# An attention, Fourier and feed-forward kernel on one core: value rows copied by ScalarE or VectorE, with a new order of all steps

## The chip, the core and the metric

The kernel runs on one core of one Trainium2 chip. The metric is the device time of one execution in microseconds (us); the time before is the median of three runs. Each engine (TensorE, VectorE, ScalarE, GpSimd, and SyncE, which issues most transfers) has its own instruction stream, and the streams meet only where one waits for another's result.

## The reference, cut to what is computed

```python
def _attn_ref(q, k, v):                      # q, k, v: (8, 8, 576, 64) float32
    scores = scale * np.matmul(q, k.transpose(0, 1, 3, 2))
    mask = (rel >= 0) & (rel < 64)           # each row sees its last 64 positions
    ...                                      # softmax
    return np.matmul(attn, v).astype(np.float32)

def _moe_ref(x, w_ch1, w_ch2):               # x: (8, 576, 512), weights float64
    X = np.fft.fft(np.fft.fft(x, axis=1), axis=2)
    u = x + np.real(X).astype(np.float32)
    ...                                      # un: u, normalized over its last axis
    ch = np.maximum(un @ w_ch1, 0.0) @ w_ch2   # 512 to 2048 and back to 512
    return (u + ch).astype(np.float32)
```

## The kernel before

The 4608 rows are cut into 36 tiles of 128 rows (T = 0 to 35, nine to a pair of batches). Each tile goes through attention (`attn_tile`); when the four and a half tiles of a batch are done, `fft` transforms that batch, `norm_tile` gathers the transformed rows, adds and normalizes them, and `ffn` and `ffn7` run the two feed-forward products on chunks of two tiles (c = 0 to 17). Tiles 0 to 12 (`T < PRO`, in the code `whole`) do attention in float32; later tiles split each float32 into two float16 parts. The weights come as float64 and are loaded, converted and squared (`weight_piece`), then scaled and split.

In attention a row sees only 64 positions, so each tile needs its own value rows and those of the tile before. There are two buffers `va` (`vbuf[0:2]`) that hold a tile's 128 value rows as loaded, each with 65 columns a head (64 values and a one), and two buffers `ve` (`vbuf[2:4]`): `v_own` (L624) copies the first 64 partitions of `va` to the tile's `ve`, and `v_next` (L632) copies the last 64 partitions to the `ve` of the next tile. One such copy is 64 partitions by 520 float32. Both are issued by SP as transfers for all tiles; for tile 12, `v_next` is two VectorE operations (L629, L630) that also split into parts. The products with the values (L739, `pa`) read `va` and `ve`.

Every step is recorded with `op(engine, duration, due time, function, reads, writes, alt=...)`. Nothing is emitted then: `Plan.follow` walks the list `ORDER`, which names all 3,023 steps by number, and this order is the order of each engine's stream. Where a step has an alternative engine (`alt`), it takes the second one if its number is in the set `SECOND`. So the two tables are a schedule written out by hand, and an engine that meets a step whose data are late holds all steps behind it. Where the plan foresees that TensorE will stand for over 0.8 us before the feed-forward products, dummy matmuls are put in (`warm`, L1551).

Names that the prediction uses: L516 loads of query, key and value rows (`qn`, `kn` in a ring of two buffers, `va`); L553 their transposes on TensorE; L486, L490, L496 helpers that copy or add on ScalarE, VectorE or any engine; L685 the exponentials on ScalarE; L1078 the gather; L1093 the first step of the normalization (`stats`); L1290 and L1271 the first and second feed-forward product of the float16 chunks and the one float32 chunk; L1299 and L1302 the two halves of the evacuation between them (ScalarE, then VectorE).

Of the kernel before, what the change touches and what calls it, by code (L numbers as in the profile page):

```python
# [382 lines left out]
def attn_fft_ffn_kernel(ctx: ExitStack, tc: tile.TileContext, q, k, v, w1, w2, gidx, dft_d, dft_s, mask, out):  # L383
# [116 lines left out]
    def attn_tile(T, base):  # L500
# [125 lines left out]
        def v_next():  # L626
# [4 lines left out]
            else:  # L631
                nc.sync.dma_start(vbuf[3 - i][64:128], vbuf[i][64:128])  # L632

        op("DMA", 0.55, base - 4 if whole else base + 3.2, v_own, [Bva[i]], [Bve[i]], lat=2.8)
        if n + 1 < NT and T + 1 == PRO:
            op("DVE", 1.1, base + 6, v_next, [Bva[i]], [Bve[1 - i]])
        elif n + 1 < NT:
# [945 lines left out]
```

## Time and profile before

| | us |
|---|---|
| median of 3 runs (lowest to highest) | 983.53 (983.04 to 984.14) |
| profiled execution | 983.49 |
| its span, first to last instruction | 981.7 |
| TensorE busy | 950.0 |
| VectorE busy | 740.5 |
| ScalarE busy | 395.6 |
| GpSimd busy | 350.4 |

The profile is one execution. A busy share counts instructions that work; the granted clock is the TensorE clock that the chip allowed, as a share of 2.4 GHz (1.00 and 0.50 are its two levels). The chain of waits is followed back from the last instruction: at each step to what released it. A table of windows gives each engine's busy time in stretches of the span, counted from its start.

### The profile page before, as it was taken

The numbers are of one execution on the slowest core, as the hardware profiler recorded it, in microseconds if no ns is written. First come the engines' busy times: TensorE is split into PE (matmuls) and PEld (weight loads), VectorE is DVE, ScalarE is ACT, GpSimd is POOL, SyncE is SP. The second block draws the span as 40 slices with busy tenths as digits, with TensorE's granted clock in tenths as the row PEclk, the third lists the DMA queues.
The fourth block names the chain that finished last, engine by engine and source line by source line (L and its number), as shares of the span: only waits on it lengthen the run. The fifth ranks groups of instructions, "written<-read, shape, count | busy, mean of one in ns | idle before, by whom it ended". The sixth has DMA issues, their size and how long they took to land.

```text
span 981.7 us, 23698 instructions
## 1 busy us (share of the span) xinstructions
PE 950.0 (97%) x9259; PEld 707.4 (72%) x9259; DVE 740.5 (75%) x2036; ACT 395.6 (40%) x895; POOL 350.4 (36%) x684
## 2 busy tenths in 40 slices
PE   7789999999999999999999899999999999999997
PEld 6566768666776767666776567666776668888887
DVE  4789898989768677765765758777889999774645
ACT  4555566843452244333442224323442324232321
POOL 0254133344452552525542223334353323232221
PEclk9899999999999999999999899999999999999999
DMA  8978764625779848699668638567863500211100
GB/s 183 214 215 237 190 192 119 152 66 109 167 169 169 156 104 159 141 177 159 135 154 144 129 86 145 122 146 154 153 123 86 104 12 28 63 36 50 25 23 23
DMA packets 309073, 123.16 MB, mean 125 GB/s; under 512 B 291096, under 2 KB 291224, under 8 KB 308960
## 3 DMA queue, kind: packets, MB, share of 16 engines
q1 hardware_dynamic: 306240, 112.72, 54.0%
q0 software_dynamic: 2720, 8.92, 3.3%
q8 instruction: 73, 1.20, 0.5%
q14 instruction: 40, 0.33, 0.1%
HBM read 54.99 MB, written 14.17 MB: 70 GB/s over the span
## 4 chain that ended last, share of the span: by engine, by line
PE 74%; DVE 10%; DMA 8%; POOL 4%; issue 2%; ACT 1%; SPq 1%; DVEq 0%; POOLq 0%; ACTq 0%
PE ph L1290 24%; PE po L1271 24%; PE ph L1429 7%; PE po L1415 7%; PE pa L739 2%; PE pz L1004 2%; PE pg L970 2%; PE psc L660 2%; DMA kn<-in_k 2%; DMA qn<-in_q 2%; DMA uhl<-up 1%; DVE td L1364 1%; DMA py<-yp 1%; POOL fs L496 1%; PE pp L696 1%
## 5 line engine op out<-in xcount | busy, mean ns | idle before, releaser
L1290 PE MATMUL ph<-uhl,w0s 128*128 128x256 f16 (+1 forms) x2616 | 331.1, 278 | 5.7 <-DVE hh L1302 4.7
L1271 PE MATMUL po<-w1s,hh 128*128 128x512 f16 (+1 forms) x1312 | 334.1, 391 | 1.8 <-DVE hh L1302 0.9
L1290 PEld LDWEIGHTS <-w0s 128*128 128x128 f16 x2496 | 243.8, 98 | 66.8 <-issue 7.1
L1271 PEld LDWEIGHTS <-hh 128*128 128x128 f16 x1248 | 119.6, 98 | 108.6 <-issue 2.2
L1299 ACT ACTIVATE hh<-ph 128x512 f16<-128x512 f32 x104 | 61.7, 595 | 174.5 <-PE ph L1290 122.5
L1302 DVE SCALAR_TENSOR_TENSOR hh<-ph,hh 128x512 f16<-128x512 f32 x104 | 71.2, 685 | 43.0 <-ACT hh L1299 42.8
L685 ACT ACTIVATE pr<-pr,nm 128x128 f32<-128x128 f32 x288 | 90.9, 390 | 24.0 <-DVE nm L677 23.9
L1429 PE MATMUL ph<-uhl,w0s 128*128 128x256 f16 x768 | 90.4, 273 | 0.2 <-DVE hh L1302 0.2
L677 DVE CUSTOM_DVE_ANT_0 pr<-psc,mskb 128x128 f32<-128x128 f32 x288 | 65.5, 284 | 25.8 <-PE psc L660 14.3
L1429 PEld LDWEIGHTS <-w0s 128*128 128x128 f16 x768 | 75.1, 98 | 10.1 <-issue 0.6
L496 POOL TENSOR_TENSOR flex<-pr,flex 128x128 f16<-128x128 f32 x88 | 41.8, 503 | 72.2 <-ACT flex L486 36.4
L1102 POOL TENSOR_TENSOR rs<-mv,mhalf 128x1 f32<-128x1 f32 x36 | 24.6, 684 | 117.7 <-DVE mv L1098 112.9
L1078 POOL DMA_INDIRECT mt<-md,gix x34 | 35.7, 1050 | 81.9 <-DMA md<-mp 28.3
L496 POOL TENSOR_TENSOR flex<-qn,flex 128x128 f16<-128x128 f32 x96 | 43.5, 486 | 18.6 <-ACT flex L486 10.4
L1415 PEld LDWEIGHTS <-hh 128*128 128x128 f16 x448 | 43.8, 98 | 5.1
L496 POOL TENSOR_TENSOR up<-un,up 128x128 f16<-128x128 f32 x64 | 29.8, 492 | 43.7 <-ACT up L486 26.5
L1440 ACT ACTIVATE hx<-ph 128x512 f32<-128x512 f32 x32 | 19.0, 596 | 60.9 <-PE ph L1429 46.4
L739 PE MATMUL pa<-ve,pt 128*64 128x65 f16 (+1 forms) x760 | 41.4, 207 | 1.5 <-DMA ve<-va 1.0
L739 PE MATMUL pa<-va,pt 128*64 128x65 f16 (+1 forms) x760 | 41.5, 207 | 0.0
L1453 DVE TENSOR_TENSOR hl<-hx,hh 128x896 f16<-128x896 f32 x27 | 29.4, 1092 | 13.2 <-ACT hh L486 12.7
L1445 DVE TENSOR_TENSOR hx<-hx 128x128 f32<-128x128 f32 x96 | 25.0, 303 | 18.7 <-ACT hx L1440 17.8
L496 POOL TENSOR_TENSOR hs<-h,hs 128x97 f16<-128x97 f32 x48 | 21.7, 484 | 47.9 <-ACT hs L486 40.5
(207 smaller groups left out, 1608.5 us busy)
## 6 DMA issues: line engine op xcount, KB each, us to landing
wd<-in_moe_w_ch SPq DMA_DIRECT2D x20, 512.0 KB, 4.7
out<-xu SPq DMA_DIRECT2D x36, 256.0 KB, 2.4
ve<-va SPq DMA_DIRECT2D x67, 130.0 KB, 3.5
kn<-in_k SPq DMA_DIRECT2D x32, 256.0 KB, 3.6
qn<-in_q SPq DMA_DIRECT2D x32, 256.0 KB, 4.2
flex<-in_moe_w_ch SPq DMA_DIRECT2D x12, 512.0 KB, 7.6
flex<-in_v SPq DMA_DIRECT2D x20, 256.0 KB, 3.3
md<-mp SPq DMA_DIRECT2D x24, 192.0 KB, 2.2
```

The lines of the kernel that those rows point to most:

```text
L496: eng.tensor_tensor(out=out[:, k : k + w], in0=in0[:, k : k + w], in1=in1[:, k : k + w], op=al)
L677: nc.vector.tensor_tensor_reduce(out=t["pr", g][:, hp], in0=t["ps", g][:, hp], in1=mskb[:, m : m + P], scale=-0.125, scalar=3.0e38, op0=AL ...
L685: nc.scalar.activation(pr, pr, AF.Exp, bias=t["nm", g][:, hp : hp + 1], scale=-1.0)
L739: nc.tensor.matmul(pa[sl, hp], pt[:, sl], v_, start=(x == 0), stop=(x == len(mm) - 1))
L1078: nc.gpsimd.indirect_dma_start(out=mts[T], out_offset=None, in_=mds[pb][0 : HR if n < 4 else 2 * HR], in_offset=bass.IndirectOffsetOnAxis( ...
L1271: nc.tensor.matmul(t["po"][i], l_, r_, start=(f == 0 and x == 0), stop=(f == NKF - 1 and x == len(mm) - 1))
L1290: nc.tensor.matmul(ph, l_, r_, start=(x == 0), stop=(x == len(mm) - 1))
L1299: nc.scalar.activation(t["hh", j][:, 0], ph, AF.Relu)
L1302: nc.vector.scalar_tensor_tensor(out=hh[:, 1], in0=ph, scalar=0.0, in1=hh[:, 0], op0=ALU.max, op1=ALU.subtract)
L1415: nc.tensor.matmul(t["po", bk][:, x], t["h", j][a][:, slot], right(n, j, b_), start=(j == 0 and k == 0 and n in (1, 7, 2, 5)), stop=(j == ...
L1429: nc.tensor.matmul(ph, l_, r_, start=(x == 0), stop=(x == len(mm) - 1))
L1453: eng.tensor_tensor(out=lo[:, a:b_], in0=x[:, a + 1 : b_ + 1], in1=hi[:, a:b_], op=ALU.subtract)
```

## The change

The 13 own copies and the 11 next copies of the float32 tiles that were transfers become steps of ScalarE, with VectorE as the alternative engine. The copies of the float16 tiles (43) stay transfers, and so do the loads.

```diff
-        op("DMA", 0.55, base - 4 if whole else base + 3.2, v_own, [Bva[i]], [Bve[i]], lat=2.8)
+        if whole:
+            op("ACT", 0.62, base - 4, lambda e: copy(e, vbuf[2 + i][0:64], vbuf[i][0:64]), [Bva[i]], [Bve[i]],
+               alt=("DVE", 0.36))
+        else:
+            op("DMA", 0.55, base + 3.2, v_own, [Bva[i]], [Bve[i]], lat=2.8)
         if n + 1 < NT and T + 1 == PRO:
             op("DVE", 1.1, base + 6, v_next, [Bva[i]], [Bve[1 - i]])
+        elif n + 1 < NT and whole:
+            op("ACT", 0.62, base - 3.9, lambda e: copy(e, vbuf[3 - i][64:128], vbuf[i][64:128]), [Bva[i]], [Bve[1 - i]],
+               alt=("DVE", 0.36))
         elif n + 1 < NT:
-            op("DMA", 0.55, base - 3.9 if whole else base + 6, v_next, [Bva[i]], [Bve[1 - i]], lat=2.8)
+            op("DMA", 0.55, base + 6, v_next, [Bva[i]], [Bve[1 - i]], lat=2.8)
```

`ORDER` and `SECOND` are replaced as a whole by tables from another search, in which transfers come late twice as often and long. The number of steps and their numbering stay. Of the 24 copies two are in the new `SECOND` (179, the next copy of tile 0, and 228, the own copy of tile 2); 22 are on ScalarE. 188 other steps change their engine, among them two key copies (tiles 0 and 3) to VectorE and three copies of transposed probabilities (tiles 0 and 3) to ScalarE before the first feed-forward matmul. The gather of tile 20 that the prediction speaks of is step 1324.

In the new list the first copies stand on ScalarE so, with the steps right behind them: own copy of tile 0, exponentials of tile 0; own copy of tile 3, exponentials of tile 3; next copies of tiles 4 and 3, exponentials of tile 4; own copy of tile 5, key copy of tile 6. Ahead of the first feed-forward matmul (step 369) the two lists hold the same 71 steps of TensorE; SP has 66 steps there before and 51 after.

## Rows read from the trace of the kernel before

**Rows 1.** The page: span; busy time and share of each engine; TensorE in 40 slices.
```profile
span 981.7 us, 23698 instructions
PE 950.0 (97%) x9259; PEld 707.4 (72%) x9259; DVE 740.5 (75%) x2036; ACT 395.6 (40%) x895; POOL 350.4 (36%) x684
...
PEclk9899999999999999999999899999999999999999
```

**Rows 2.** Windows: length, busy us of each engine (x instructions), granted clock, DMA share, GB/s.
```profile
0.00:90.00 90.00, 71.37 (x845) 56.11 (x845) 66.18 (x251) 48.09 (x129) 28.69 (x65) 0.92 0.88 218
90.00:130.00 40.00, 39.74 (x279) 28.16 (x280) 35.79 (x107) 23.70 (x66) 13.87 (x23) 1.00 0.70 186
130.00:500.00 370.00, 368.46 (x3632) 262.69 (x3631) 289.00 (x814) 167.76 (x378) 157.84 (x328) 1.00 0.69 144
500.00:560.00 60.00, 54.81 (x516) 37.71 (x514) 36.38 (x92) 16.20 (x38) 18.47 (x32) 0.94 0.70 140
560.00:955.00 395.00, 393.82 (x3797) 303.45 (x3796) 300.19 (x745) 136.16 (x281) 127.12 (x231) 1.00 0.41 86
955.00:982.00 27.00, 21.80 (x200) 19.29 (x198) 12.98 (x29) 3.69 (x6) 4.45 (x7) 0.97 0.06 21
```

**Rows 3.** Groups of TensorE: busy us, mean ns | idle before them.
```profile
L1551 PE MATMUL warm<-ident 128*128 128x256 f16 x87 | 15.1, 310 | 2.2 <-POOL ident masks.py:199 2.2
```

**Rows 4.** Chain of waits up to 130 us: start us, length us, what.
```profile
7.52 3.56 DMA kn<-in_k
...
11.87 5.74 DMA qn<-in_q
...
18.80 5.94 DMA qn<-in_q
...
26.16 0.44 SPq L632
26.60 0.04 issue
26.65 3.53 DMA ve<-va
30.18 0.14 issue
...
31.24 3.52 DMA qn<-in_q
...
36.58 9.93 DMA kn<-in_k
...
90.19 1.99 PE ph L1290 x8
```

**Rows 5.** Windows of 5 us, columns as in rows 2.
```profile
75.00:80.00 5.00, 4.64 (x26) 2.94 (x24) 4.90 (x25) 3.30 (x12) 1.48 (x3) 1.00 1.11 310
90.00:95.00 5.00, 4.80 (x24) 4.27 (x25) 5.00 (x8) 2.42 (x8) 4.19 (x6) 1.00 0.62 168
545.00:550.00 5.00, 4.94 (x18) 2.60 (x18) 4.93 (x9) 0.00 (x0) 4.83 (x7) 0.50 0.41 81
```

**Rows 6.** Chain of waits, 500 to 552 us.
```profile
511.55 1.31 PE ph L1290 x12
512.86 1.29 PE po L1271 x6
...
533.96 6.74 DMA mt<-md,gix
...
545.06 2.72 PE ph L1290 x12
547.77 2.56 PE po L1271 x6
```

**Rows 7.** Timelines of VectorE and TensorE: start, length, what [idle before, releaser].
```profile
540.72 0.68 DVE L1093 TENSOR_TENSOR xu<-xu,mt 32x512 f32<-32x512 f32 x1 [4.21 <-DMA mt<-md,gix]
...
545.06 2.72 PE L1290 MATMUL ph<-uhl,w0s 128*128 128x256 f16 x12 [4.28 <-DVE hh L1302]
```

**Rows 8.** Transfers issued up to 90 us: count, KB each, median us to landing.
```profile
ve<-va SPq DMA_DIRECT2D x15, 130.0 KB, 3.7
va<-in_v SPq DMA_DIRECT2D x7, 256.0 KB, 6.9
```

**Rows 9.** Groups of ScalarE and VectorE up to 230 us, and the one line L629.
```profile
L486 ACT CAST up<-un 128x512 f16<-128x512 f32 x5 | 3.1, 619 | 6.6 <-issue 4.5 <-DVE un L1106 2.0
...
L490 DVE COPY pt<-pp 128x512 f32<-128x512 f32 x4 | 2.7, 684 | 2.8 <-PE pp L696 2.8
...
L629 DVE TENSOR_SCALAR ve<-va x1: 428/428/428, 230.2 to 230.2; 64x520 f16<-64x520 f32 x1
```

**Rows 10.** Waits of SP's queue up to 130 us: us in total, times, longest.
```profile
SPq L624 <- DMA va<-in_v: 6.2, 3, 3.2
SPq L632 <- DMA va<-in_v: 3.6, 1, 3.6
SPq L632 <- PE pa L739: 2.7, 1, 2.7
```

**Rows 11.** Timeline of VectorE: its first instruction.
```profile
9.31 0.29 DVE L677 CUSTOM_DVE_ANT_0 pr<-psc,mskb 128x128 f32<-128x128 f32 x1 [9.31 <-PE psc L655]
```

**Rows 12.** Timeline of ScalarE around 541 us: start, length, what [idle before].
```profile
540.96 0.62 ACT L486 CAST flex<-pr 128x512 f16<-128x512 f32 x1 [9.53 <-DMA pt<-flex]
541.48 1.08 ACT L1299 ACTIVATE hh<-ph 128x512 f16<-128x512 f32 x2
```

262 rows, old and new, of tables (ORDER, SECOND) are left out of this document.

## The prediction

> **What bounds the kernel now.** I read the page's busy shares first: TensorE works 97% of the span [rows 1], so only the time in which it stands, turns dummy matmuls or runs at the half clock can be won. The table of windows shows where that is [rows 2]: before 90 us TensorE works 71.4 of 90 us, and 15.1 us of matmul time are the kernel's own dummies [rows 3]; from 90 to 130, 130 to 500 and 560 to 955 us it stands 0.3, 1.5 and 1.2 us in all; from 500 to 560 us it stands 5.2 us, and the last 27 us hold 5.2 us of ending that the change does not touch. So two places matter.
>
> The first is the stretch up to the first feed-forward matmul at 90.19 us. The chain of waits, read in order of time [rows 4], is five loads of key and query rows from 7.5 to 46.5 us with one value copy among them (0.44 us of issue on SP and 3.53 us to land). The loads land in 3.5 to 9.9 us. Later VectorE carries the chain: it is busy 4.90 of 5 us from 75 to 80 and 5.00 from 90 to 95 [rows 5].
>
> The second is one stall [rows 5 to 7]. A gather issued at 533.96 us lands after 6.74 us; VectorE stands 4.21 us for it, and the evacuation of the feed-forward product (L1302) stands behind it in VectorE's order, so TensorE stops for 4.28 us. The granted clock is 0.50 from 545 to 550 us, the lower level: two groups take 2.72 and 2.56 us that take 1.31 and 1.29 elsewhere. In all 4.3 + 2.7 = 7.0 us.
>
> **The change part by part.**
>
> Transfers leave. 13 own and 11 next copies go, 24 in all. Counting along the two order tables, 15 of them lie before the first feed-forward matmul, as the profile has it too: 15 of 130 KB [rows 8], 2.0 of the 19.6 MB moved by 90 us, 10%. The set of TensorE steps ahead of that matmul is the same 71 in both tables, so a shorter stretch is a shorter kernel.
> - The one value copy on the chain: -(0.44 + 3.53) us, and in its place one engine copy. The trace has no float32 copy between these buffers; the nearest rows are 0.62 us for a 128x512 cast on ScalarE and, on VectorE, 0.43 us for a 64x520 operation of the same value rows, up to 0.68 us for a 128x512 copy [rows 9]. I take 0.62, with 0.15 us for the hand-over seen as "issue" ahead of a chain step. -3.2 us; bounds -3.5 and 0 (if another transfer ends last there).
> - Traffic: the five loads on the chain take 28.7 us; at most a tenth of that, 2.9 us, goes with a tenth of the bytes, at least none. I take 1.5.
> - SP's queue: copies waited there for value loads and for TensorE 6.2 + 3.6 + 2.7 = 12.5 us up to 130 us [rows 10], and loads queued behind them waited too. Most of these loads also wait for one of two key/query buffers to be free, so I take 0.5 us and bound it by 0 and 2.
>
> Work arrives on the engines. The two lists put 22 copies on ScalarE and 2 on VectorE. Up to the first feed-forward matmul ScalarE gets 12 of them and a net of one more PSUM copy, 12 x 0.62 + 0.6 = 8.0 us on an engine that is busy 48.1 of 90 us [rows 2]: cover enough, and if the cover is gone each costs its 0.62 us in line. VectorE gets two copies, two key copies, two weight conversions and one copy of transposed rows (seven), and gives up three PSUM copies, one radix step and one normalization; seven that come and five that go, of about the size of the 0.43 and 0.68 us in rows 9 but for the radix step, so I put this at nothing, within 0.7 us.
>
> A new wait comes with them: a copy now waits for its value load in ScalarE's order, where exponentials and PSUM copies stand behind it. In the chosen case it is never last; the last rival prices it.
>
> Sum up to the first feed-forward matmul: -3.2 - 1.5 - 0.5 = -5.2 us at the fifth tile. Not all of it arrives: VectorE has 66.2 us of work before 90 us [rows 2] and starts at 9.3 us [rows 11], so it is idle 14.5 us after that; each us won must come out of that, while weights still have to be loaded. I keep two thirds, -3.5 us; bounds -8.4 (3.5 + 2.9 + 2, all kept) and 0.
>
> The table. All engines' lists are reshuffled and 188 further steps change engine, so single waits after 130 us can't be followed one by one. What can be counted is how much TensorE work lies between a transfer's issue and the first matmul that needs the evacuation queued behind the transfer's user on ScalarE or VectorE (1.31 and 1.29 us a group [rows 6]). In the old table 5 places have under 7 us of it, the least 5.6; in the new one none has, the least 7.3. At the stalled gather the old order left six groups, 7.8 us; the new one leaves seven groups and two small ones, 9.9 us, and a cast that ran ahead of the evacuation comes after it (0.34 us). If the gather lands as late again, the stall is 4.3 - 2.1 - 0.3 = 1.9 us, a gain of 2.4; if the clock then also stays up, 5.1. Against that, other places can turn late. I take -3.0; bounds -7.0 and +3.2, the price of one new stall like this one with half its clock loss beside the gain of 2.4 (4.3 + 1.3 - 2.4).
>
> In total -3.5 - 3.0 = **-6.5 us**. The profiled execution took 983.49 us around its span of 981.7, equal to the median of 983.53 within 0.04, so the forecast is 983.5 - 6.5 = **977.0 us**, its own range 971 to 981.5.
>
> A rule that speaks against the ScalarE choice: the rows show 0.62 us for a cast of 512 columns there and 0.43 us for the 520-column operation on VectorE [rows 9]. The Trainium skill (ScalarE: Activation LUTs, Rules for kernel authors) tells to give multiplications, additions and the like to VectorE, as the faster one per element. By the rule the 12 early copies would cost 12 x 0.19 = 2.3 us less engine time; by the windows they would lie on the engine that carries the chain, 12 x 0.43 = 5.2 us longer, so here the rows go against the rule.
>
> **The rivals.**
> - All terms in full: the early bound -8.4 and the whole stall -7.0 give 968.1 us. For it: the loads on the chain are long because they share the engines with other transfers. Against it: VectorE must find 8.4 in its 14.5 idle us.
> - Hidden anyway: the value copies mostly ran beside other transfers (one of 15 is on the chain), VectorE's stretch absorbs what they free, and the new table trades one stall for another. 0 us, 983.5. For it: a query and a key load come right after the copy on the chain and may end last instead. The Trainium skill (DMA: Bandwidth & Descriptors, Rules for kernel authors) advises to issue a transfer early and wait late so that its fixed cost overlaps with compute. By that rule a copy that was already overlapped gives nothing back, and the trace shows one of 15 that was not [rows 4].
> - Slower: ScalarE's order is held by late value loads. The profile has this shape once [rows 12]: a cast waited 9.53 us for a transfer, and the evacuations behind it came after it. Value loads land in 6.9 us [rows 8]. The new table puts the first copy of tiles 3, 4 and 5 only 2.3, 3.5 and 1.7 us of TensorE work behind its load; with 71.4 - 15.1 = 56.3 us of real work in 90 us that is 3.7, 5.6 and 2.7 us of time. Held 6.9 - 3.7, 6.9 - 5.6 and 6.9 - 2.7 us: 8.7 us, with the exponentials of tiles 3 and 4 behind. Less the 3.2 us of the copy on the chain and the 2.4 us at the stalled gather: +3.1, 986.6 us. It decides from landings of about 4 us on; below that it costs nothing. Against it: loads should land sooner with a tenth less traffic, and the old order held SP, with loads behind, for the same landings.
>
> **How the numbers follow.** The forecast has 0.50, all in full 0.12, hidden 0.14, slower 0.24. Faster by over 0.2% (2 us, about what a measurement of this kernel can tell from no change) is 0.50 + 0.12 = 0.62; within it 0.14; slower 0.24. The range goes from 968 (just past the full case) to 987 (just past the slower case), which leaves out half of the slower case and a few hundredths below: 0.15 in all.
>
> **What would show it.** Right: the first feed-forward matmul (L1290) starts about 86.5 instead of 90.2 us; no value copy (ve<-va) in the chain before it; key and query loads on it nearer 3.6 us; 43 of the 67 value copies by transfer left; TensorE idle under 3 us between 500 and 560 us. Wrong: long idle of ScalarE ahead of the new copies with the value load as releaser, or exponentials (L685) late on the chain; the first feed-forward matmul still at 90 us with VectorE at 5 of 5 us before it; or a new stall of several us after 130 us with a granted clock of 0.5 behind it.

## The result and the profile after

The changed kernel takes 972.38 us (median of four runs, 971.87 to 973.33) beside 983.28 us (four runs, 981.28 to 984.14) of the kernel before on the same chip: a ratio of 0.9893, 95% interval 0.9876 to 0.9910, 10.9 us less. The forecast was 977.0 us, 6.5 us less, with a range of 968 to 987.

The profiled execution took 973.33 us, its span 971.6 us. The page's busy shares and the slices of the granted clock of the changed kernel, beside [rows 1]:

```profile
span 971.6 us, 23675 instructions
PE 945.1 (97%) x9262; PEld 705.1 (73%) x9262; DVE 739.3 (76%) x2038; ACT 408.8 (42%) x919; POOL 344.2 (35%) x682
...
PEclk9989999999999999999999999999999999999999
```

ScalarE gained 13.2 us of work, VectorE lost 1.2, and the slice of the clock that was low at about 545 us is gone. Where the time went is in the table of windows of the changed kernel, columns as in [rows 2] (its last boundary lies 10 us earlier, as the kernel is shorter):

```profile
0.00:90.00 90.00, 72.30 (x864) 58.06 (x865) 69.28 (x255) 56.63 (x143) 32.27 (x70) 0.94 0.78 204
90.00:130.00 40.00, 40.00 (x284) 29.18 (x283) 32.97 (x108) 25.42 (x68) 10.66 (x17) 1.00 0.75 215
130.00:500.00 370.00, 369.30 (x3644) 262.16 (x3643) 287.25 (x810) 174.43 (x393) 165.91 (x351) 1.00 0.69 138
500.00:560.00 60.00, 60.00 (x568) 41.77 (x567) 42.72 (x112) 17.45 (x40) 14.38 (x24) 1.00 0.74 146
560.00:945.00 385.00, 383.33 (x3724) 296.07 (x3723) 293.27 (x727) 130.37 (x271) 121.02 (x221) 1.00 0.41 85
```

Between 500 and 560 us TensorE now works 60.00 of 60 us at full clock; it worked 54.81 at a mean of 0.94. Ahead of 90 us the DMA share fell from 0.88 to 0.78.

To compare kernels the rest of this text cuts each trace at two points of TensorE's timeline: the start of the first feed-forward product (the first matmul into ph) and the end of the last matmul. The stretch ahead is the start, the stretch between them the middle, what is left of the span the end.

| | start | middle | end | span |
|---|---|---|---|---|
| before | 90.19 | 886.61 | 4.90 | 981.7 |
| changed | 86.88 | 878.29 | 6.43 | 971.6 |
| difference | -3.3 | -8.3 | +1.5 | -10.1 |

So in this pair of profiles a third of the gain is in the start and the rest in the middle, and the ending gave 1.5 us back. The chain of waits of the changed kernel up to the first feed-forward product (start us, length us, what), beside [rows 4]:

```profile
8.21 3.69 DMA qn<-in_q
...
19.44 5.25 DMA qn<-in_q
...
31.84 6.05 DMA flex<-in_moe_w_ch
...
86.95 1.92 PE ph L1297 x8
```

Six transfers became three, no value copy is among them, and a weight load has come in. The new copies in the groups of ScalarE up to 230 us (count, busy us, mean ns, then the idle time ahead and its releasers), and the page's line of the copies that are still transfers (count, KB, median us to landing), beside [rows 8, 9]:

```profile
L486 ACT COPY ve<-va 64x520 f32<-64x520 f32 x22 | 13.6, 622 | 1.7 <-PE psc L662 1.3 <-PE pa L746 0.2
...
ve<-va SPq DMA_DIRECT2D x43, 130.0 KB, 2.8
```

622 ns each, and ScalarE stood 1.7 us in all ahead of 22 copies, 1.5 of it for results of TensorE, so at most 0.2 us for value loads. In VectorE's timeline the gathered rows that stalled it before are used without a wait (a wait would stand in brackets, as in [rows 7]), 4.7 us after GpSimd issued the gather. The last line is that gather among the transfers (count, us from issue to landing; it was 6.74 in [rows 6]):

```profile
524.78 1.01 POOL L1085 DMA_INDIRECT mt<-md,gix  x1 [3.39 <-DVE xu L1100]
...
529.52 0.67 DVE L1100 TENSOR_TENSOR xu<-xu,mt 32x512 f32<-32x512 f32 x1
...
mt<-md,gix POOLq DMA_INDIRECT x1, 4.6
```

So two things differ. The new order lets VectorE come to the gathered rows later, 4.74 us after the issue, where in the old order it stood ready after 2.55 us (540.72 less 4.21 of waiting, less 533.96). And the gather itself lands 2.1 us sooner, which no step of the prediction has.

### The profile page after: what moved, and what is told of

It is laid out like the page before. It is cut to its first block, busy times and chain, and to the rows that moved or that the text cites. A ratio compares the mean times of both kernels' runs of the same rounds, so it can differ in the third digit from the quotient of the medians.

```text
span 971.6 us, 23675 instructions
## 1 busy us (share of the span) xinstructions
PE 945.1 (97%) x9262; PEld 705.1 (73%) x9262; DVE 739.3 (76%) x2038; ACT 408.8 (42%) x919; POOL 344.2 (35%) x682
## 4 chain that ended last, share of the span: by engine, by line
PE 87%; DVE 7%; POOL 2%; DMA 2%; issue 1%; ACT 1%; SPq 0%; POOLq 0%; DVEq 0%
PE ph L1297 29%; PE po L1278 29%; PE ph L1436 8%; PE po L1422 7%; PE pa L746 3%; PE pz L1011 3%; PE psc L667 2%; PE pg L977 2%; DVE td L1371 1%; PE psc L662 1%; DMA qn<-in_q 1%; PE pp L703 1%; POOL fs L496 1%; DVE y L496 1%; DMA flex<-in_moe_w_ch 1%
## 5 line engine op out<-in xcount | busy, mean ns | idle before, releaser
L1309 DVE SCALAR_TENSOR_TENSOR hh<-ph,hh 128x512 f16<-128x512 f32 x104 | 71.4, 686 | 51.4 <-ACT hh L1306 50.7
L1452 DVE TENSOR_TENSOR hx<-hx 128x128 f32<-128x128 f32 x108 | 28.4, 305 | 33.9 <-ACT hx L1447 33.0
L496 POOL TENSOR_TENSOR flex<-pr,flex 128x128 f16<-128x128 f32 x72 | 35.6, 526 | 51.5 <-ACT flex L486 39.5
L496 POOL TENSOR_TENSOR flex<-qn,flex 128x128 f16<-128x128 f32 x96 | 43.3, 487 | 28.0 <-ACT flex L486 24.2
L496 POOL TENSOR_TENSOR up<-un,up 128x128 f16<-128x128 f32 x60 | 27.0, 479 | 38.0 <-ACT up L486 19.6
L496 POOL TENSOR_TENSOR y<-xu 128x128 f32<-128x128 f32 x40 | 19.6, 521 | 50.1 <-DVE xu L756 45.1
L1422 PE MATMUL po<-w1s,hh 128*128 128x256 f16 x192 | 34.7, 273 | 0.0
```

Source lines behind the costliest of these rows:

```text
L496: eng.tensor_tensor(out=out[:, k : k + w], in0=in0[:, k : k + w], in1=in1[:, k : k + w], op=al)
L1309: nc.vector.scalar_tensor_tensor(out=hh[:, 1], in0=ph, scalar=0.0, in1=hh[:, 0], op0=ALU.max, op1=ALU.subtract)
L1422: nc.tensor.matmul(t["po", bk][:, x], t["h", j][a][:, slot], right(n, j, b_), start=(j == 0 and k == 0 and n in (1, 7, 2, 5)), stop=(j == ...
```

## The experiments

The theory on record has two parts that add up: copies that leave the transfers shorten the start, the new table removes the stall at 540 us. A first rival says that the table does everything; a second that what counts is not the copy's landing but what the transfers did to others: by bytes, by SP's issues, or by the waits that hold SP. Each chip's runs are compared with runs of the kernel before on the same chip, by their ratio. All kernels at a glance; start, middle and end are from one profile each, and the profiled execution lies up to 3.6 us off the kernel's median (984.25 for the table alone, 973.72 for the last but two):

| kernel | median us | ratio to before (95%) | start | middle | end |
|---|---|---|---|---|---|
| table alone, copies by transfer | 987.80 | 1.0062 (1.0040 to 1.0083) | 95.89 | 880.5 | 6.1 |
| copies alone, old table | 974.30 | 0.9926 (0.9902 to 0.9949) | 85.46 | 881.1 | 5.4 |
| before, one evacuation ahead | 979.82 | 0.9986 (0.9971 to 1.0000) | 87.66 | 883.8 | 4.9 |
| changed, old order after 210 us | 977.40 | 0.9947 (0.9928 to 0.9966) | 87.97 | 884.5 | 5.4 |
| changed, again | 971.78 | 0.9893 (0.9872 to 0.9914) | 84.74 | 878.9 | 6.4 |
| changed + 130 KB transfers, no wait | 977.25 | 0.9950 (0.9932 to 0.9968) | 89.16 | 879.5 | 5.9 |
| changed + 130 KB transfers, with wait | 978.37 | 0.9973 (0.9953 to 0.9992) | 91.22 | 879.3 | 6.1 |
| changed + 1 KB transfers, no wait | 978.72 | 0.9970 (0.9954 to 0.9985) | 91.09 | 881.6 | 5.9 |
| changed + 1 KB transfers, with wait | 983.11 | 1.0004 (0.9984 to 1.0024) | 96.10 | 879.3 | 6.0 |
| copies early in old order, new order late | 970.51 | 0.9875 (0.9857 to 0.9893) | 84.49 | 881.5 | 5.8 |
| before, new order after 210 us | 976.10 | 0.9949 (0.9929 to 0.9969) | 87.69 | 879.5 | 5.6 |
| changed, all copies on VectorE | 974.10 | 0.9925 (0.9902 to 0.9947) | 87.81 | 879.1 | 5.9 |

### The table alone

The new tables, with all copies as transfers at their places in the new list:

```diff
-        if whole:
-            op("ACT", 0.62, base - 4, lambda e: copy(e, vbuf[2 + i][0:64], vbuf[i][0:64]), [Bva[i]], [Bve[i]],
-               alt=("DVE", 0.36))
-        else:
-            op("DMA", 0.55, base + 3.2, v_own, [Bva[i]], [Bve[i]], lat=2.8)
+        op("DMA", 0.55, base - 4 if whole else base + 3.2, v_own, [Bva[i]], [Bve[i]], lat=2.8)
...
```

> The changed kernel's two order tables, but the 24 copies stay transfers issued by SP, each at the copy's place in the list. Theory 'table': the gain is the new order's alone, the stall at 540 us is gone (-7.9 us) and the start gains its 3.2 us too, 972 to 973 us, first feed-forward matmul near 87 us. Theory 'transfers': the 3.2 us of the start need the copies off the transfers; only the stall goes, 975.5 us, first feed-forward matmul at 89 to 91 us, value copies back in the chain before it.

987.80 us, slower than before: the table by itself loses 0.62%. Neither theory had a loss. The middle (880.5 us) is nearly as short as in the changed kernel (878.3 and 878.9), but the start is 95.89 us, 9 us longer. TensorE's waits and SP's waits up to 130 us in this kernel (total us, times, longest):

```profile
PE pa L736 <- DMA ve<-va: 6.1, 2, 3.7
...
SPq L513 <- DMA ve<-va: 10.3, 4, 4.1
```

The new list puts a tile's copy close ahead of its use. As a transfer it is then late for TensorE, and the next load into the same value rows waits in SP's queue until the copy has read them: 10.3 us, where the kernel before had 0.2 us of such waits and 1.0 us of TensorE's. So the two parts of the change can't be reckoned apart: this table wants a copy that is done after 0.62 us.

### The copies alone

The changed code with both tables of before (the first line of ORDER stands for them), so that all 24 copies go to ScalarE:

```diff
 ORDER = [int(i) for i in """
-171 9 2 1 7 8 172 10 0 173 174 175 3 196 176 177 197 180 178 11 181 199 185 182 198 179 201 186 200 183 222 202 187 12
+171 9 2 8 1 7 172 0 173 174 175 3 197 176 177 196 180 178 181 11 185 182 199 179 186 183 200 198 201 184 202 187 222
...
```

> The 24 copies on ScalarE, but the old tables. Theory 'transfers': the start gains 2 to 4 us by itself (first feed-forward matmul at 86 to 88 us) and the stall at 540 us stays, 980 us. Theory 'table': no gain, first feed-forward matmul at 90 us, 983 us. Rival 'ScalarE held': a copy in ScalarE's stream waits for its value load with exponentials behind it; over 984 us, with idle time of ScalarE ahead of the copies.

974.30 us, 0.74% or 7.3 us less than before: most of the gain without any new order, and more than either theory had. The start is 85.46 us. And the stall did not stay, although the order is the old one. The window of 500 to 560 us, VectorE's step on the gathered rows and the gather's landing (as above):

```profile
500.00:560.00 60.00, 59.16 (x558) 40.70 (x556) 42.02 (x111) 18.69 (x40) 21.46 (x38) 1.00 0.70 151
...
533.15 0.68 DVE L1097 TENSOR_TENSOR xu<-xu,mt 32x512 f32<-32x512 f32 x1 [2.34 <-DMA mt<-md,gix]
...
mt<-md,gix POOLq DMA_INDIRECT x1, 4.7
```

The gather lands after 4.7 us, VectorE waits 2.34 us for it, and TensorE stands 0.8 us at full clock. So the old order makes the wait, and how late the gather lands makes its length: where it landed after 6.74 us, TensorE stood 4.28 us. By this profile part of the copies' gain lies in the middle (881.1 us for 886.6). The copies by engine are worth 7.3 us in the old order, and 16.6 us in the new one (1.0062 to 0.9893).

### The changed kernel again, with the removed transfers' burdens put back

Three kernels on one chip: the changed one unedited, and two with 24 transfers beside the engines' copies that nobody waits for. They bring back 130 KB each, first from a table in DRAM, without a wait:

```diff
+        def also(e, out, in_, x):
+            copy(e, out, in_)
+            junk = dr.tile([64, H * 65], F32, tag=f"jk{T}{x}", name=f"jk{T}{x}", bufs=1)
+            nc.sync.dma_start(junk, dft_s.bitcast(F32)[64 * x : 64 * x + 64, 0 : H * 65])
...
```

and then from the value rows, so that SP waits for their load as the old copies did:

```diff
-            nc.sync.dma_start(junk, dft_s.bitcast(F32)[64 * x : 64 * x + 64, 0 : H * 65])
+            nc.sync.dma_start(junk, in_)
```

> The changed kernel, unedited, beside the three others of this chip. Both theories: 972 to 974 us, ratio 0.989 to 0.991 to the kernel before. A second profile of it tells how much its start moves from run to run: the first feed-forward matmul was at 86.95 us in the first profile.

> The changed kernel with 24 transfers of 130 KB added that nobody waits for, issued by SP without a wait where the engines' copies stand in the table: the bytes and SP's issues of the removed copies are back, their late landing on the path is not. Theory that the gain comes from traffic (the 1.5 us of the forecast) and SP's issues (0.5 us): 1.5 to 3 us slower than the changed kernel, 974.5 to 976. Theory that the gain is only the landing of a copy ahead of its user: within 0.7 us of the changed kernel.

> As the run before, but the added transfers read the value rows, as the removed ones did, so that SP also waits for each value load before it issues one and holds the loads queued behind it. Theory that SP's queue, held by these waits, is the larger part: 2 us or more slower than the kernel with the transfers that do not wait, 977 to 980 us. Theory that it is traffic or landing: within 1 us of that kernel.

971.78, 977.25 and 978.37 us. What the transfers do to others is thus worth 5.5 us and more, over half of the gain, although the copies on the path are still ScalarE's; the forecast had 2.0 us for it. Whether SP's waits add to it can't be told from the last two, whose intervals overlap. A second profile of the changed kernel starts at 84.74 us against 86.88 in the first: one profile's start is known to some 2 us. Kernels of the table that share the list up to the last value copy show the same: old list with transfers 90.19, 87.66 and 87.69, changed list 86.88, 84.74 and 87.97, old list with engine copies 85.46 and 84.49. By the means of these, the changed start is 2.0 us shorter than before, and not 3.3.

### Bytes or issues

The same two kernels with 16 bytes of each row in place of 2,080:

```diff
-            junk = dr.tile([64, H * 65], F32, tag=f"jk{T}{x}", name=f"jk{T}{x}", bufs=1)
-            nc.sync.dma_start(junk, dft_s.bitcast(F32)[64 * x : 64 * x + 64, 0 : H * 65])
+            junk = dr.tile([64, 4], F32, tag=f"jk{T}{x}", name=f"jk{T}{x}", bufs=1)
+            nc.sync.dma_start(junk, dft_s.bitcast(F32)[64 * x : 64 * x + 64, 0:4])
```

```diff
-            nc.sync.dma_start(junk, dft_s.bitcast(F32)[64 * x : 64 * x + 64, 0:4])
+            nc.sync.dma_start(junk, in_[:, 0:4])
```

> The changed kernel with 24 added transfers of 64 rows of 16 bytes, from DRAM to DRAM, that nobody waits for and that wait for nothing: SP's issues and the rows to be described are back, the bytes are not. Theory that the bytes in flight cost the time (the two kernels with 130 KB each took 977.3 and 978.4): within 1 us of the changed kernel, 971.5 to 973. Theory that SP's issues cost it: 3 to 5 us slower, 975 to 977.

> As the run before, but the 16 bytes of each row are read from the value rows, so that SP waits for each value load before it issues and holds the loads queued behind. Theory that SP held by waits is a term of its own: 1 to 3 us slower than the run before it. Theory that it is only bytes: within 1 us of it, 971.5 to 973.

978.72 and 983.11 us. These ran on another chip than the three above, so the ratios compare them: without the bytes the loss to the changed kernel is 0.77% (7.6 us), no smaller than the 0.57% with them, so the theory of the bytes falls. With the wait it is 1.11% (10.9 us): all that the changed kernel had won. Both are above what was expected; the intervals of the two just touch, so the size of the wait's share (0.34%) is not settled. By the profiles most of the loss lies in the start: 6.4 of 8.6 us without the wait, all of it with the wait. The windows of the first 40 us, the changed kernel (run again) first, the one with small transfers without a wait second, columns as in [rows 2]:

```profile
0.00:40.00 40.00, 29.48 (x427) 23.74 (x428) 29.07 (x131) 27.77 (x68) 12.34 (x31) 1.00 0.90 224
```

```profile
0.00:40.00 40.00, 28.73 (x399) 23.04 (x400) 23.36 (x110) 22.87 (x56) 8.38 (x25) 0.91 0.81 182
```

In the second the DMA engines are less busy (0.81 for 0.90) and move less (182 for 224 GB/s): bandwidth is not what the loads lack. They are issued late, and the four weight loads (wd) of this stretch also take longer to land, 7.6 us for 5.2 (medians), while the key loads take 3.2 in both. SP's timeline of the second kernel shows the issues (start us, length us, what; jk are the added transfers):

```profile
15.33 1.37 SPq L516 DMA_DIRECT2D va<-in_v  x1
17.20 0.37 SPq L516 DMA_DIRECT2D kn<-in_k  x1
17.62 2.52 SPq L637 DMA_DIRECT2D jk<-in_dft_s  x1
20.19 0.58 SPq L1182 DMA_DIRECT2D wd<-in_moe_w_ch  x1
20.82 0.50 SPq L637 DMA_DIRECT2D jk<-in_dft_s  x1
21.42 0.53 SPq L516 DMA_DIRECT2D qn<-in_q  x1
22.26 0.37 SPq L516 DMA_DIRECT2D va<-in_v  x1
22.68 3.42 SPq L1182 DMA_DIRECT2D wd<-in_moe_w_ch  x1
26.20 1.37 SPq L516 DMA_DIRECT2D qn<-in_q  x2
27.62 1.13 SPq L637 DMA_DIRECT2D jk<-in_dft_s  x1
29.05 1.29 SPq L516 DMA_DIRECT2D kn<-in_k  x2
30.38 1.54 SPq L637 DMA_DIRECT2D jk<-in_dft_s  x2
31.96 0.58 SPq L1182 DMA_DIRECT2D flex<-in_moe_w_ch  x1
```

SP goes from one issue to the next nearly without a gap: 15.6 of 17.2 us are issues. Over the first 32 us its issues fill 26.3 us here and 24.2 us with the added transfers of 130 KB, beside 20.5 and 18.4 us in the changed kernel's two profiles and 21.1 us in the kernel before. The seven jk up to here take 7.2 us of it (the four lines of jk above hold five, 5.69 us, and two stand earlier, 0.91 and 0.59 us). The same weight load, the first into flex, is issued at 25.76 us in the changed kernel's second profile:

```profile
25.76 0.62 SPq L1177 DMA_DIRECT2D flex<-in_moe_w_ch  x1
```

It is 6.2 us earlier, and the first feed-forward product 6.4 us earlier (84.74 for 91.09); in the first profile, at 27.15 us, it is 4.8 us earlier, and the product 4.2 us. Adding up SP's issues in the timeline up to 90 us gives 47.35 us in 68 entries for the kernel before, 15 of them value copies of 10.72 us in all, 39.3 us in 56 entries for the changed one (36.1 in its second profile), and 49.3 and 51.4 us with the added transfers of 1 KB and of 130 KB without a wait. In the kernel with small transfers that wait, SP's queue shows up to 130 us:

```profile
SPq L516 <- DMA jk<-va: 9.0, 4, 3.9
SPq L637 <- DMA va<-in_v: 6.9, 3, 2.7
```

The second line is the old copies' wait for their load (6.2 + 3.6 us in [rows 10]), the first the next load's wait for the copy's reading, as in the table alone.

What stays open is the part of the 1 KB transfers that the DMA engines, not SP, make costly: each adds as many packets as one of 130 KB does (306,240 in all on both pages), and lands hardly sooner or even later, after 5.2 us for 6.0 from DRAM and 4.5 us for 4.0 from the value rows (medians). The Trainium skill (DMA: Bandwidth & Descriptors, Specifications) says that pieces under 512 bytes are done as read-modify-write; these two pairs differ in direction and don't show it. Copies of the old kind, from SBUF to SBUF and without a wait, weren't tried.

### One evacuation moved ahead

To see whether the order alone makes the stall, two steps of the kernel before, the halves of the evacuation that stood behind the late gather, go ahead of the gather's user:

```diff
-1402 1597 2400 1325 1459 2398 1555 2402 1659 2401 1321 2399
+1402 1597 2400 2398 2399 1325 1459 1555 2402 1659 2401 1321
```

> The kernel before with two steps moved in its list: the two halves of one feed-forward evacuation (steps 2398 on ScalarE and 2399 on VectorE) go ahead of the normalization of tile 20 (1325) that waits for the late gather and of the cast that waits for a late transpose. Theory 'held behind a late transfer': TensorE no longer stops at 540.8 us for 4.3 us and the clock stays up, 976 to 978 us. Rival 'late anyway': the next evacuation or the attention of tile 26 stops TensorE instead, 981 to 983 us.

979.82 us, a ratio of 0.9986 (0.9971 to 1.0000): 1.4 us by the ratio, barely told from nothing. VectorE's timeline of this kernel shows why:

```profile
533.86 0.68 DVE L1299 SCALAR_TENSOR_TENSOR hh<-ph,hh 128x512 f16<-128x512 f32 x1
538.50 0.68 DVE L1090 TENSOR_TENSOR xu<-xu,mt 32x512 f32<-32x512 f32 x1 [3.96 <-DMA mt<-md,gix]
...
544.71 0.68 DVE L1299 SCALAR_TENSOR_TENSOR hh<-ph,hh 128x512 f16<-128x512 f32 x1
```

The moved evacuation (533.86 us) is early, the gather is as late as before (3.96 us of waiting for 4.21), and now the next evacuation comes only at 544.71. The window of 500 to 560 us:

```profile
500.00:560.00 60.00, 55.50 (x531) 37.97 (x529) 39.96 (x106) 17.09 (x40) 18.37 (x32) 1.00 0.71 140
```

4.5 us still idle, now at full clock. The late transfer moved the stall to what stood next; this one change of place did not cure it.

### Where in the list the new order gains

Three kernels join the lists behind step 746, the last value copy of the change (190 us in the old list, 210 us in the new). The changed kernel with the old order behind it:

```diff
-712 486 2062 746 736 751 2063 713
+712 486 2062 746 756 736 713 751
...
```

> The changed kernel's list up to its last copy (tile 12, some 210 us), then all remaining steps in the old order with the old engines. Theory 'two separate places': the start's 3.2 us come and the stall near 537 us comes back whole, 980 us. Rival 'the stall is chance of timing': with everything 3 us earlier the transfers fall otherwise and the stall is smaller or gone, 973 to 976 us.

977.40 us, between the two theories. From here to the changed kernel (0.9947 to 0.9893) the new late order is worth 0.54%, 5.3 us. Its window of 500 to 560 us has part of the stall back; VectorE waits 2.57 us for a gather that lands after 4.9:

```profile
500.00:560.00 60.00, 56.92 (x532) 38.74 (x530) 40.67 (x111) 17.75 (x40) 19.28 (x33) 0.97 0.72 149
```

The kernel before, its transfers included, with the new order behind:

```diff
-475 476 467 746 2042 468 477 775
+475 476 467 746 775 2042 2040 468
...
```

> The kernel before with its own table and its transfers up to the last value copy that the change touches (about 210 us), and the new table's order behind that. Theory that the new order gains late, with or without engine copies, and that what it loses with transfers is all in the start: 977 to 980 us, the first feed-forward matmul where the kernel before has it, TensorE idle under 1.5 us between 500 and 560 us. Theory that the late stall goes with the early traffic and not with the order: within 1 us of the kernel before, 981 to 983 us.

976.10 us, 0.51% less than before with no engine copy at all. In its window of 500 to 560 us the stall is gone (1.3 us idle, and no wait for the gather, which lands after 4.0):

```profile
500.00:560.00 60.00, 58.70 (x559) 40.86 (x558) 41.60 (x110) 15.62 (x35) 14.94 (x26) 1.00 0.76 146
```

And this list with all 24 copies on ScalarE:

```diff
+        if whole:
+            op("ACT", 0.62, base - 4, lambda e: copy(e, vbuf[2 + i][0:64], vbuf[i][0:64]), [Bva[i]], [Bve[i]],
+               alt=("DVE", 0.36))
...
```

> The old table up to the last value copy (about 210 us) with all 24 copies on ScalarE, and the new table's order behind it. Theory that the copies' engine carries the early gain and the new order the late one, each by itself: the first feed-forward matmul near 85.5 us, no stall from 500 to 560 us, 971 to 973.5 us, as fast as the changed kernel or faster. Theory that the new table's early order is worth something by itself beside engine copies: 974 to 976 us, the first feed-forward matmul 1 to 3 us later than in the changed kernel.

970.51 us, 0.9875 (0.9857 to 0.9893), the lowest median of all. The changed kernel's interval overlaps it (0.9872 to 0.9914), so it isn't shown to be the faster one. The gains add up: copies alone -0.74%, new late order alone -0.51%, both -1.25%. The new early order beside engine copies gives nothing that can be told: +0.18% from this kernel to the changed one, +0.21% from the copies alone to the changed kernel with the old late order, both within the intervals. Beside transfers it costs 1.13% (0.9949 to 1.0062). In all, TensorE idles 0.8 to 5.2 us between 500 and 560 us in the four profiles with the old late order, and 0 to 1.3 us in those with the new one.

### All copies on VectorE

The set SECOND of the changed kernel, which holds two of the 24 copies, gets the numbers of the other 22:

```diff
 SECOND = {int(i) for i in """
+178 203 204 229 253 254 278 279 494 495 519 520 544 545 569 671 672 696 697 721 722 746
...
```

> The changed kernel with all 24 copies on VectorE (in it 22 are on ScalarE). The forecast reckoned that the 12 early copies would make the engine that carries the chain 12 x 0.43 = 5.2 us longer; of this two thirds would arrive: 3 us or more slower than the changed kernel, 975 to 977. Theory that VectorE has room for them and the rule of the faster engine holds: within 1 us of the changed kernel, 971 to 973.

974.10 us, 0.9925 (0.9902 to 0.9947), 0.32% or 3.1 us above the changed kernel by the ratios; the intervals just overlap, so the sign is likely and the size is not settled. This lies between the two theories. The copies in VectorE's list of this kernel (ns: least, median, most; first and last start):

```profile
L488 DVE COPY ve<-va x24: 406/428/673, 7.6 to 212.2; 64x520 f32<-64x520 f32 x24
```

Most are shorter than on ScalarE (median 428 ns for 622; the longest, 673, is not). VectorE's busy time before 90 us is 72.83 us, where it was 69.28, and the start is 87.81 us against 86.88 and 84.74; that the one makes the other is argued, as the starts lie within what profiles differ. The rule of the Trainium skill that the prediction weighed (ScalarE: Activation LUTs, Rules for kernel authors) gives `add` and `mul` to VectorE as the faster engine; VectorE is the faster one for this copy too, and the times lean against its use here.

## Why the prediction came out as it did, step by step

The sign and the range held; the size was 6.5 us forecast and 10.9 measured. By steps:

- **The copy on the chain, -3.2 us.** As a row it went as forecast: no value copy is on the chain ahead of the first feed-forward product. But the chain was not the old one less a link: of five key and query loads two are left, and a weight load is there instead (in the second profile two such loads, 3.64 and 5.13 us, and no weight load). The step's price can't be checked by itself.
- **Traffic, -1.5 us.** Not borne out. Transfers of 1 KB cost as much as those of 130 KB (0.9970 and 0.9950 of before).
- **SP's queue, -0.5 us, bounded by 2.** This is the step of the start that failed. The reason given was that most loads behind a value copy also wait for a buffer. What it left out is that each issue takes SP's own time and puts the later loads off: its issues fill 21.1 of the first 32 us in the kernel before, and 26.3 us with the small transfers. Issues put back cost 7.6 us (with what the DMA engines themselves make of 1 KB transfers, above), issues with their waits 10.9 us, in the new order. The prediction read the waits of [rows 10] and not SP's own issue time, which its timeline had shown: 10.7 us of 47.
- **Two thirds kept, -3.5 us in the start.** 90.19 to 86.88 is -3.3, -5.5 by the second profile, and -2.0 by the means given above. That the first pair comes so near is luck: the traffic was put too high and SP's queue too low.
- **Work on ScalarE and VectorE.** As forecast: 622 ns a copy for 0.62, and cover enough. (Ahead of the first feed-forward step the new list has 14 of the 24 copies, 12 and 2, and only the old one 15.) VectorE is nearly full now: 28.15 of 30 us busy between 30 and 60 us, where it was 22.18. What the prediction did not look at is GpSimd: its additions (L496) carry the chain of waits from 41.44 to 61.83 us but for one cast on ScalarE, and from 53.67 to 67.27 us in the kernel before; 6.35 and 5.25 us of these GpSimd stands. Which of the two engines holds back the rest of what SP gives back was not tried.
- **The table, -3.0 us.** The counting was right, and the premise that the gather lands as late again failed. It counted 2.1 us more TensorE work behind the gather's issue, and VectorE comes to the gathered rows 2.2 us later after it (4.74 for 2.55). But the gather landed after 4.6 us for 6.7; with 6.7 VectorE would still have waited some 2.0 us (an estimate from these two numbers), the 1.9 of the reckoning. As it landed sooner and the clock stays at 1.00, the whole went: 5.19 us of idle TensorE and the low clock (54.81 us at 0.94, 3.3 us), 8.5 us together, as the middle's -8.3 has it. What sets the landing was not tried: it was 4.7 to 7.1 us in the four profiles with the old late order and 3.4 to 4.8 us in the ten with the new one. Over many runs the late order is worth 5.0 to 5.3 us (0.51% and 0.54%): the stall of the one profile on which the forecast stood was larger than that.
- **The ending, taken as untouched.** It grew by 1.5 us (0.7 to 1.5 in the kernels with the new late order). VectorE's last step ends 2.2 us after the last matmul, where it was 1.5, and the span ends 4.2 us after that, where it was 3.4. The new table reorders this part too, and nothing in the prediction stood for that.
- **The sum.** It treated copies and table as two terms side by side. For the late order that is right (-0.74 and -0.51 make -1.25%). For the early order it is not: without engine copies the same table is 0.62% slower than before. And the copies alone are worth 7.3 us, where the forecast gave them 3.5; this is the larger part of what the sum missed.

**The rivals.** "All in full" (968.1) came nearest in mechanism: the whole stall went, though its early part was 3.3 or 5.5 us in the two profiles and not its 8.4. "Hidden anyway" is out. "Slower" named the right danger, copies too close behind their loads, on the wrong engine: ScalarE waited at most 0.2 us for value loads, but with transfers just this made the table alone slower.

**What would show it.** The first feed-forward product came at 86.88 for 86.5 us; 43 copies by transfer are left; TensorE is idle 0.0 us between 500 and 560. The query loads on the chain are 3.69 and 5.25 us, so only one is near 3.6.

## What to carry to other kernels

A queue that issues transfers is an engine: add up its issue times in the stretch that matters, as one does for the others, before putting a price on bytes or on the landing of the one transfer that stands on the chain. Moving a small copy to an idle engine paid here by the issues and waits that left the queue, and a schedule made for the short copy can lose with the long one, so copy and schedule belong together. A stall behind a late transfer is to be priced with the chance that the transfer lands sooner and the stall goes in full, and not from one profile alone: here one gather landed after 3.4 to 7.1 us from kernel to kernel.

## What the runs showed of the hardware

- SP's time for an issue is not fixed: the added 24 transfers of 1 KB took from 0.50 to 2.52 us each, with a median of 0.59, and in the same stretch of the same kernel a weight load took 3.42 us. What sets it isn't settled by these runs.
- The 43 copies between SBUF buffers that remain as transfers land in 2.8 and 3.0 us in the two profiles of the changed kernel, and the same 43 in 3.1 us before (medians behind 210 us). The 3.5 us on the page of the kernel before is that of all 67.
- The same operation, 64x520 float32, takes 622 ns on ScalarE and 428 ns on VectorE (medians), with single ones up to 673 ns on VectorE.
